# Batch 3's attention begins three steps earlier, and the last output tile is copied by one engine

## The chip, the cores and the metric

The kernel runs on one core of a Trainium2 chip. A core has five engines with a queue each: TensorE (PE in the profile, with PEld for its weight loads), VectorE (DVE), ScalarE (ACT), GpSimd (POOL) and SyncE (SP), which here issues nearly all DMAs. The metric is the device time of one execution in microseconds; shorter is better. What a measurement of this kernel can tell from no change is about 0.2%, some 1.7 us.

## The reference

Three layers in a row: an attention with landmarks (Nystrom) on 4 batches, then two feed-forward layers over 2304 tokens, all in float32.

```python
B, H, S, D = 4, 8, 576, 64              # m = 32 landmarks
q_lm = q.reshape(B, H, m, S // m, D).mean(axis=3)   # k_lm likewise
A, Bm, C = sm(q, k_lm), sm(q_lm, k_lm), sm(q_lm, k) # scaled softmaxes
Z = Bm.T / (norm1(Bm) * norminf(Bm) + 1e-6)
for _ in range(6):
    Z = 2 * Z - Z @ Bm @ Z
x = A @ Z @ C @ v                        # -> 2304 x 512
h = x @ w_in;  x = silu(h) @ w_out       # moe:  512 -> 2048 -> 512
xn = x / rms(x) * rms_g                  # moe2: 512 -> 1536 -> 512
out = (silu(xn @ w_gate) * (xn @ w_val)) @ w_out2
```

## The kernel before

**Precision.** Most matrices are held as a rounded upper part and a remainder (`split`: a cast on ScalarE, a subtraction on VectorE), and one product takes three matmuls.

**First part: 128 steps.** Batch 0 takes steps 0 to 31, and batches 1 to 3 take 32 each: two halves of 288 tokens by 16 blocks of 128 hidden units. A step `i` computes one block's hidden values (`moe1_h`: six matmuls into `h`, then Silu into `s` and the split into `hl`), and three steps later (`LAG`) `retire` multiplies them by the output weights into four PSUM banks `a` (`moe1_out`, twelve matmuls). At the end of a half `moe1_sum` copies these four banks out (tiles `e` and `ex`, by VectorE and ScalarE in turn) and stores them in `x2T`.

**Attention beside it.** While batch b is in its steps, the attention of batch b+1 runs in small pieces, one per step: the generator `attend(ap, b)` lets group 0 (four heads) run alone for `LONE[b]` steps, then both groups together, then six rounds of the iteration for Z (`pe`), then a last small product `pl`, which gives `lts[b]`. `attention(ap, b, g)` holds the pieces of one group; the number of bare `yield`s after `landmarks(kT)` puts off its scores (`pq`, `c1`, `c2`). With `lts[b]` there, `wprime(b, n)` multiplies a quarter n of the input weights by it (`pw` into `wp`), which `moe1_h` uses; it also starts the load of the quarter two further on (`win` from `wind`) into the tile just read. The four `wp` tiles that batch 3's quarters need come free after steps 83, 87, 91 and 95, and a step makes at most one quarter, so each is made in the first such step from the end of the attention on.

**Preparation of the second part.** When the last attention is done, its memory is closed and the pool `p2` opened in its place; the generator `pre` then prepares eight of the twelve weight blocks of the second layer, in the order 1 to 7, 0: load `fw` from `w2d`, four sums `t4` (VectorE), splits into one single-buffered tile `w7p` (ScalarE and VectorE), stores to `w7d` and `wod`. A block takes 12 ticks, and a step gives 2.5 ticks, up to step 125 (the loop's `PRE_REST`); what is left is emitted after the loop (`finish(pre)`). Block 0 is not reloaded: the first step of the second part multiplies by `w7p` itself. Beside it `conversion` turns raw float64 weights into `w2d` (until about step 94).

**Second part: 36 steps.** `moe2_step` does seven products of six matmuls (`ga`, `gb`, `gc`), and between them the output products `o` of the step before (`out_tile`), with weights `oc` loaded by `load_wo2`; `load_split` loads the block `w7` of a later step, `load_f32` the raw block `fw` of one that `late` prepares (8 to 11). The last step's six tiles are copied from PSUM and stored by `out_tile` and `store_out`.

The order of instructions on each engine is made by the framework's scheduler from the order of the code, priorities and buffers, so a moved generator also moves others.

Of the kernel before, what the change touches and what calls it, by code (L numbers as in the profile page):

```python
# [18 lines left out]
P = 128  # L19
B, H, S, D = 4, 8, 576, 64  # L20
# [3 lines left out]
DM = H * D  # L24
# [7 lines left out]
TB = 384  # L32
# [35 lines left out]
LOAD_AT = {3: "o8", 4: "o9", 5: "o10", 6: "n30", 7: "n31", 8: "o11", 9: "o12", 10: "o13", 11: "o14", 12: "o15"}  # L68
CONV_AT = {5: "n20", 6: "n21", 7: "o4", 8: "o5", 9: "o6", 10: "o7", 11: "n30", 12: "n31",
           13: "o8", 14: "o9", 15: "o10", 16: "o11", 17: "o12", 18: "o13", 19: "o14", 20: "o15"}  # L70
NEXT, NEXT0 = 5, 13
FAST_AT = 20
PRE_N = 8
PRE_STEPS, PRE_RATE = 12, 2.5
# [2 lines left out]
NORM_END = 9  # L77
XSPLIT = (0, 3, 6, 9, 12, 15, 18)
LOW = 9
LONE = (0, 6, 8, 8)  # L80


@with_exitstack
def nystrom_moe_kernel(ctx: ExitStack, tc: tile.TileContext, q, k, v, w_in, w_out, w_gate, w_val, w_out2, rms_g, out):
    nc = tc.nc
    PE, DVE, ACT, POOL, SP = nc.tensor, nc.vector, nc.scalar, nc.gpsimd, nc.sync
# [68 lines left out]
    def nslot(i, name, shape, dt=F32):  # L155

        return nw.tile(list(shape), dt, tag=f"n{i}", name=name, bufs=1)
# [54 lines left out]
    def tile_at(n):  # L212
        return (n + NF - CUT) % NF
# [89 lines left out]
    class Queue:  # L303

        last = {}
# [372 lines left out]
    def attention(ap, b, g):  # L678


        n = f"{b}_{g}"
# [35 lines left out]
        yield  # L717
        landmarks(kT)
        yield
        for _ in range((0, 0, 2, 1)[b]):  # L720
            yield

        sa = ht("sa", [P, R, M])
# [29 lines left out]
        with tc.issue_after(now[-1][0].ins):  # L753
            x = AE.activation(ec[:, w1:], c2[:, :nc2], AF.Exp, bias=nb[:, 0:1], scale=0.125 / R, accum_out=su[:, 1:2])
# [9 lines left out]
        last = VE.transpose(bb[:, 1], bb[:, 0])  # L764
# [48 lines left out]
    def attend(ap, b):  # L813


        gens = [attention(ap, b, g) for g in range(NG)]
        for _ in range(LONE[b]):
            next(gens[0])
# [38 lines left out]
    def wprime(b, nb_, prio=0):  # L857


        t = wslot(f"wp_{b}_{nb_}", [P, NG, 2, 512], F32R)  # L860
        pw = [ps(f"pw_{b}_{nb_}_{g}") for g in range(NG)]
        x = []
        if b == 0:
            x = [h_mm[0], *(win_ins["W{0}{1}0"] + win_ins["W{0}{1}1"] if nb_ == 0 else [win_ins[g, nb_] for g in range(NG)])]
        for i in range(4):
            for g in range(NG):
                hr = slice(64 * g, 64 * g + 64)
                with ExitStack() as es:
                    es.enter_context(tc.high_priority(offset=prio))
                    for y in x:  # L870
                        es.enter_context(tc.issue_after(y.ins))
                    PE.matmul(pw[g][32 * i:32 * i + 32], lts[b][hr, i], win_t[i // 2, nb_][hr, i % 2], start=True, stop=True)  # L872
        with tc.high_priority(offset=prio):
            for g in range(NG):
                x = ACT.copy(t[:, g, 0], pw[g])
                y = DVE.tensor_tensor(t[:, g, 1], pw[g], t[:, g, 0].bitcast(F32), op=ALU.subtract)
        wpr[b, nb_] = t

        if b and (b < B - 1 or nb_ < 2):
            n = (nb_ + 2) % 4  # L880
            for g in range(NG):
                win_t[g, n] = nslot(2 * (n % 2) + g, f"win_{g}_{n}_{b}", [P, 2, 512])
                SP.dma_start(out=win_t[g, n].rearrange("p c f -> p (c f)"), in_=wind[g, n])
        return x, y
# [148 lines left out]
    def moe1_h(b, hf, f, c):  # L1033
        ph = ps(f"h_{b}_{hf}_{f}", [P, HB])
        nb_, fo = f // 4, (f % 4) * P
        tk = slice(HB * hf, HB * hf + HB)
        i = 0
        for g in range(NG):
            w, a = wpr[b, nb_][:, g], at_t[b, g]
            for (x, y) in ((0, 0), (0, 1), (1, 0)):  # L1040
                h_mm[0] = PE.matmul(ph, w[:, x, fo:fo + P], a[:, y, tk], start=i == 0, stop=i == 5)  # L1041
                i += 1
        if whole(b, hf, c):
            s = hp.tile([P, 2, HB], F32, tag="hl", name=f"s_{b}_{hf}_{f}")[:, 0]
            x = QA.activation(s, ph, AF.Silu) if f >= NF - CUT else ACT.activation(s, ph, AF.Silu)
            return s, (x, x)
        s = st.tile([P, HB], F32, tag="s", name=f"s_{b}_{hf}_{f}")
        ACT.activation(s, ph, AF.Silu)  # L1048
        hl = hp.tile([P, 2, HB], F32R, tag="hl", name=f"hl_{b}_{hf}_{f}")
        return hl, split(hl, s, lo=DVE)  # L1050
# [126 lines left out]
    def store_out(e, row, last):  # L1177

        for h in range(2):
            y = slice(64 * h, 64 * h + 64)  # L1180
            (SP, POOL)[h and last].dma_start(out=out[row + 64 * h:row + 64 * h + 64], in_=e[y])

    nx = {}

# [80 lines left out]
    oacc = {}  # L1265

    def out_tile(prev, n):

        if prev is None:
            return  # L1270
        p, f, hls, w = prev
        j, t = 1 - n // 3, n % 3
        if f == 0:
            oacc[n] = po.tile([P, DM], F32, tag="o", name=f"o_{p}_{n}", bufs=6)
        for i, (x, y) in enumerate(((0, 0), (0, 1), (1, 0))):
            PE.matmul(oacc[n], hls[j][:, x, t * P:(t + 1) * P], w[:, y], start=f == 0 and i == 0, stop=f == NF2 - 1 and i == 2)  # L1276
        if f == NF2 - 1:
            e = nslot(n, f"e2_{p}_{n}", [P, DM])
            row = (2 * p + j) * TB + t * P
            last = 0 if p < NB2 // 2 - 1 else 1 + n // 5  # L1280
            if last < 2:
                (DVE.tensor_copy if n % 2 else ACT.copy)(e, oacc[n])
                store_out(e, row, last)
            else:
                e2 = nslot(n + 1, f"e2_{p}_{n}_1", [P, DM])
                half = DM // 2
                for eng, fn, t, x in ((POOL, DVE.tensor_copy, e, slice(0, half)), (ACT, ACT.copy, e2, slice(half, DM))):
                    fn(t[:, x], oacc[n][:, x])
                    eng.dma_start(out=out[row:row + P, x], in_=t[:, x])

    def pg(name, tag):
        return pp.tile([P, TB], F32, tag=tag, name=name, bufs=1)
# [2 lines left out]
    def run(gens, n=1):  # L1295
        for _ in range(n):
            for gn in list(gens):
                if next(gn, gens) is gens:
                    gens.remove(gn)
# [41 lines left out]
    pend, gens = [], []  # L1341
# [3 lines left out]
    def ready(b):  # L1345
        return all((b, g) in l_t for g in range(NG))
# [17 lines left out]
    nxt = 1  # L1364
# [16 lines left out]
    for i, (b, hf, f, c) in enumerate(steps):  # L1381
        while hf == 0 and (b, f // 4) not in wpr:
            if not ready(b):
                run(gens)
            else:
                wpfree -= b > 0
                wprime(*todo.pop(0))
        hl, cuts = moe1_h(b, hf, f, c)
        pend.append((steps[i], hl))
        if i + 1 < len(HEAD):  # L1390
            go(HEAD[i + 1])
        if c and f == tile_at(NF - 1):
            es_t[b, hf, c] = sum_tiles(b, hf, c)
        now.append(cuts)
        if not gens and nxt < B and i + NEXT >= 32 * (nxt - 1) + (NEXT0 if nxt == 1 else 0):
            gens = [attend(ap, nxt)]
            nxt += 1
        if gens:
            run(gens, 2 if FAST_AT <= i < 32 else 1)
        if len(pend) > LAG:  # L1400
            retire()
        if hf == 1 and f % 4 == 3:
            wpfree += b < B - 1
        if b == 0:
            if i in LOAD_AT:
                load_job(LOAD_AT[i])
            after = wprime(*todo.pop(0), WP_PRIO) if i in WP_AT else ()
            if i in CONV_AT:
                with behind((*cuts, *after)):
                    finish(jobs.pop(CONV_AT[i]))  # L1410
            if i in KEEP_AT:
                with tc.issue_after(loads.last.ins):
                    keep_win(KEEP_AT.index(i))
        if 0 <= i - SPLIT_AT < NF:
            with behind(cuts):
                split_wout(i - SPLIT_AT)
        if todo and todo[0][0] >= max(b, 1) and ready(todo[0][0]) and wpfree and not (jobs and todo[0][0] > b):
            wpfree -= 1
            wprime(*todo.pop(0))
        if nxt == B and not gens and p2 is None:  # L1420
            att.close()
            p2 = ctx.enter_context(tc.tile_pool(name="p2", bufs=1, side="right"))
        if i >= CONV2_AT:
            due[0] += CONV2_RATE
        if p2 and i < len(steps) - PRE_REST:
            due[1] += PRE_RATE
        with tc.issue_after(cuts[0].ins), tc.issue_after(cuts[1].ins):
            for j, gn in enumerate((conv2, pre)):
                while due[j] >= 1:
                    due[j] -= 1  # L1430
                    next(gn, None)
        if p7 and 1 not in w7_t7:
            w7_t7.append(1)
            load_split(1)
        if p3x and len(x0) > 2:
            finish(norm0)
            split_x(0, x0.pop(0))
        if b == B - 1 and not todo:
            for _ in range(1 + (i % 3 > 0)):
                next(norm0, None)  # L1440
# [17 lines left out]
    for p in range(NB2 // 2):  # L1458
        nxt = p + 1 if p + 1 < NB2 // 2 else None
# [76 lines left out]
```

## Time and profile before

| | |
|---|---|
| median of 3 runs | 847.08 us (845.92 to 847.38) |
| profiled execution: its time, and the span of its instructions | 846.0 us, 843.9 us |
| PE busy | 819.6 us (97%), 6200 matmuls |
| DVE, ACT, POOL busy | 528.6 (63%), 440.3 (52%), 16.2 us (2%) |
| mean granted TensorE clock | 0.992 |
| DMA | 202.89 MB, mean 240 GB/s |

Busy times are sums over the span of 843.9 us; 2.1 us of the execution lie around it. An engine's share is an average over parts with different limits, so the parts are read one by one.

### The profile page before, as it was taken

Reading aid. Unit: us, or ns where it says so; the run is one execution under the profiler, and the core shown is the slowest. Engines: PE = TensorE matmul, PEld = TensorE weight load, DVE = VectorE, ACT = ScalarE, POOL = GpSimd, SP = SyncE. Lnnn points to the kernel's source line nnn. Section 1 sums busy time; section 2 is a strip of 40 time slices with the busy share of each in tenths; the row PEclk is TensorE's granted clock in tenths of the full one; section 3 lists DMA queues with packets and bytes.
Section 4 is the critical chain, followed back from the end, with each engine's and each line's share of the span. In section 5 each row is a group of like instructions: output and inputs, shape, how many; then the busy total and the mean of one; then the engine's idle time right before and its main releaser. Section 6 shows DMA issues by size and latency. Waiting matters only on the chain.

```text
span 843.9 us, 15909 instructions
## 1 busy us (share of the span) xinstructions
PE 819.6 (97%) x6200; PEld 737.5 (87%) x6200; DVE 528.6 (63%) x1111; ACT 440.3 (52%) x929; POOL 16.2 (2%) x46
## 2 busy tenths in 40 slices
PE   8899899999999999999799999999999999999997
PEld 5677678998899979999789999999999999999996
DVE  6988868776589758679544389743458533333332
ACT  4786755785677757667424447433345323232222
POOL 2200000000000000000000000000000000000001
PEclk9999999999999999999989999999999999999999
DMA  9989357478995678868975558668565558555542
GB/s 341 352 298 370 135 170 256 141 219 271 319 307 172 211 252 322 297 247 307 352 262 188 196 191 278 247 229 298 217 224 200 184 188 290 224 221 191 187 186 76
DMA packets 73355, 202.89 MB, mean 240 GB/s; under 512 B 6720, under 2 KB 35008, under 8 KB 69312
## 3 DMA queue, kind: packets, MB, share of 16 engines
q1 hardware_dynamic: 72848, 200.96, 66.7%
q8 instruction: 49, 0.80, 0.4%
q0 software_dynamic: 288, 0.79, 0.3%
q14 instruction: 26, 0.21, 0.1%
q10 hardware_dynamic: 144, 0.13, 0.0%
HBM read 149.29 MB, written 52.56 MB: 239 GB/s over the span
## 4 chain that ended last, share of the span: by engine, by line
PE 88%; DMA 5%; DVE 3%; ACT 2%; SPq 1%; issue 1%; POOL 0%; POOLq 0%; ACTq 0%; DVEq 0%
PE a L1061 18%; PE o L1276 18%; PE ga L1202 18%; PE h L1041 12%; PE gc L1202 9%; PE gb L1202 4%; PE a L1058 4%; PE pw L872 2%; DMA winr<-in_moe_w_in_dram 2%; DMA w7d<-w7p 1%; PE pe L318 1%; DMA win<-wind 1%; DMA fw<-w2d 1%; DMA kT<-in_k_dram 1%; PE pu L301 1%; PE pq L318 1%
## 5 line engine op out<-in xcount | busy, mean ns | idle before, releaser
L1061 PE MATMUL a<-hl,wo 128*128 128x288 f32 x1296 | 194.4, 298 | 0.0
L1061 PEld LDWEIGHTS a<-hl,wo 128*128 128x128 f32 x1296 | 177.7, 188 | 4.3 <-issue 2.1
L1276 PE MATMUL o<-oc,u 128*128 128x512 f32 x648 | 178.9, 394 | 0.0
L1202 PE MATMUL ga<-x,w 128*128 128x384 f32 x840 | 171.9, 339 | 0.0
L1202 PEld LDWEIGHTS ga<-x,w 128*128 128x128 f32 x840 | 152.1, 189 | 12.4 <-ACT a L200 0.2
L1276 PEld LDWEIGHTS o<-oc,u 128*128 128x128 f32 x648 | 119.4, 188 | 13.3 <-DVE u L165 0.3
L1041 PE MATMUL h<-at,wp 128*128 128x288 f32 x768 | 129.9, 305 | 0.2 <-DVE sa L200 0.2
L1041 PEld LDWEIGHTS h<-at,wp 128*128 128x128 f32 x768 | 111.0, 190 | 13.8 <-issue 5.9
L200 DVE TENSOR_TENSOR v<-u,gc 128x384 f32<-128x384 f32 x72 | 39.6, 551 | 124.1 <-PE gc L1202 123.9
L1202 PE MATMUL gc<-x,w 128*128 128x384 f32 x420 | 84.8, 336 | 0.0
L1048 ACT ACTIVATE s<-h 128x288 f32<-128x288 f32 x108 | 44.1, 413 | 75.5 <-PE h L1041 71.3
L1202 PEld LDWEIGHTS gc<-x,w 128*128 128x128 f32 x420 | 75.0, 188 | 2.9
L200 ACT COPY u<-ga 128x384 f32<-128x384 f32 x72 | 34.6, 480 | 73.8 <-PE ga L1202 73.6
L164 ACT CAST u<-u 128x384 fp32r<-128x384 f32 x72 | 37.0, 514 | 66.9 <-DVE u L200 66.9
L200 DVE TENSOR_TENSOR u<-z,v 128x384 f32<-128x384 f32 x72 | 40.1, 556 | 45.7 <-ACT z L200 44.4
L165 DVE TENSOR_TENSOR hl<-s,hl 128x288 fp32r<-128x288 f32 x108 | 48.7, 451 | 25.8 <-ACT hl L164 24.0
L165 DVE TENSOR_TENSOR u<-u,u 128x384 fp32r<-128x384 f32 x72 | 40.0, 556 | 27.1 <-ACT u L164 26.8
L200 ACT ACTIVATE z<-ga 128x384 f32<-128x384 f32 x36 | 17.7, 492 | 69.2 <-PE ga L1202 68.9
L164 ACT CAST hl<-s 128x288 fp32r<-128x288 f32 x108 | 46.8, 433 | 2.6
L1058 PE MATMUL a<-s,wor 128*128 128x288 f32 x160 | 42.5, 409 | 0.8 <-DVE wor L191 0.8
L1202 PE MATMUL gb<-x,w 128*128 128x384 f32 x210 | 42.5, 337 | 0.0
L1058 PEld LDWEIGHTS a<-s,wor 128*128 128x128 f32 x160 | 29.1, 189 | 10.7 <-issue 2.2
(204 smaller groups left out, 931.8 us busy)
## 6 DMA issues: line engine op xcount, KB each, us to landing
w<-w7d SPq DMA_DIRECT2D x31, 1792.0 KB, 7.5
oc<-wod SPq DMA_DIRECT2D x32, 512.0 KB, 7.9
win<-wind SPq DMA_DIRECT2D x20, 512.0 KB, 5.6
w2d<-c SPq DMA_DIRECT2D x36, 256.0 KB, 2.8
fw<-w2d SPq DMA_DIRECT2D x12, 768.0 KB, 6.2
winr<-in_moe_w_in_dram SPq DMA_DIRECT2D x8, 1024.0 KB, 8.1
wor<-in_moe_w_out_dram SPq DMA_DIRECT2D x16, 512.0 KB, 10.3
w7d<-w7p SPq DMA_DIRECT2D x16, 512.0 KB, 5.0
```

The costliest lines, as they stand in the source:

```text
L164: x = ACT.copy(dst[:, 0], src) if hi is ACT else hi.tensor_copy(dst[:, 0], src)
L165: return x, lo.tensor_tensor(dst[:, 1], src, dst[:, 0].bitcast(F32), op=ALU.subtract)
L200: self.last = getattr(self.eng, name)(*args, **kw)
L301: eng.matmul(pu[y], ct[0:VC[c], c, y], vn[0:VC[c], c, h ^ 1], start=c == 0, stop=c == 4)
L318: x = getattr(self.eng, name)(*args, **kw)
L872: PE.matmul(pw[g][32 * i:32 * i + 32], lts[b][hr, i], win_t[i // 2, nb_][hr, i % 2], start=True, stop=True)
L1041: h_mm[0] = PE.matmul(ph, w[:, x, fo:fo + P], a[:, y, tk], start=i == 0, stop=i == 5)
L1048: ACT.activation(s, ph, AF.Silu)
L1058: PE.matmul(acc[d], w[:, y], hl, start=start, stop=stop)
L1061: PE.matmul(acc[d], w[:, x, y], hl[:, z], start=start and i == 0, stop=stop and i == 2)
L1202: mm[0] = PE.matmul(acc, w7[:, x, o, kk], xs[:, y, kk], start=start and n == 0, stop=stop and n == 5, skip_group_check=True)
L1276: PE.matmul(oacc[n], hls[j][:, x, t * P:(t + 1) * P], w[:, y], start=f == 0 and i == 0, stop=f == NF2 - 1 and i == 2)
```

## The change

Batch 3's attention begins at step 56 in place of 59 (a table of starting steps replaces the rule; the entries for batches 1 and 2 are the steps that the rule gave). Its group 1 follows seven steps behind group 0, before eight, and the scores wait one more step. The last of the six output tiles of the last step is copied from PSUM by ScalarE as a whole and stored in two halves of 64 rows by SP's and ScalarE's queues; before, VectorE and ScalarE copied 256 columns each, and GpSimd's and ScalarE's queues stored them.

```diff
-NEXT, NEXT0 = 5, 13
+START = (None, 8, 27, 56)
-LONE = (0, 6, 8, 8)
+LONE = (0, 6, 8, 7)
@@ def attention(ap, b, g):
-        for _ in range((0, 0, 2, 1)[b]):
+        for _ in range((0, 0, 2, 2)[b]):
             yield
@@ def store_out(e, row, last):
-            (SP, POOL)[h and last].dma_start(out=out[row + 64 * h:row + 64 * h + 64], in_=e[y])
+            (SP, POOL, ACT)[h and last].dma_start(out=out[row + 64 * h:row + 64 * h + 64], in_=e[y])
@@ def out_tile(prev, n):
-            row = (2 * p + j) * TB + t * P
             last = 0 if p < NB2 // 2 - 1 else 1 + n // 5
-            if last < 2:
-                (DVE.tensor_copy if n % 2 else ACT.copy)(e, oacc[n])
-                store_out(e, row, last)
-            else:
-                e2 = nslot(n + 1, f"e2_{p}_{n}_1", [P, DM])
-                half = DM // 2
-                for eng, fn, t, x in ((POOL, DVE.tensor_copy, e, slice(0, half)), (ACT, ACT.copy, e2, slice(half, DM))):
-                    fn(t[:, x], oacc[n][:, x])
-                    eng.dma_start(out=out[row:row + P, x], in_=t[:, x])
+            (DVE.tensor_copy if n % 2 and last < 2 else ACT.copy)(e, oacc[n])
+            store_out(e, (2 * p + j) * TB + t * P, last)
@@ the loop over the 128 steps
-        if not gens and nxt < B and i + NEXT >= 32 * (nxt - 1) + (NEXT0 if nxt == 1 else 0):
+        if not gens and nxt < B and i >= START[nxt]:
```

Three places in the order of instructions. The first is VectorE's queue in batch 2's second half, where the first `wp` tiles of batch 3 are made (`hl_2_1_8` is step 88's, `r_` and `c_` are conversion). Before:

```order
L165 TENSOR_TENSOR hl_2_1_9_4326<-s_2_1_9_4324,hl_2_1_9_4326 128x288
L189 SCALAR_TENSOR_TENSOR r_v_11_4167<-r_v_11_4167 128x512
L191 SCALAR_TENSOR_TENSOR c_2028<-c_2028,r_v_11_4167 128x512
L876 TENSOR_TENSOR wp_3_0_4348<-pw_3_0_0_4349,wp_3_0_4348 128x512
L876 TENSOR_TENSOR wp_3_0_4348<-pw_3_0_1_4350,wp_3_0_4348 128x512
L165 TENSOR_TENSOR hl_2_1_10_4384<-s_2_1_10_4382,hl_2_1_10_4384 128x288
```

and now:

```order
L165 TENSOR_TENSOR hl_2_1_6_4241<-s_2_1_6_4239,hl_2_1_6_4241 128x288
L191 SCALAR_TENSOR_TENSOR c_31_4226<-c_31_4226,r_g_10_4075 128x512
L876 TENSOR_TENSOR wp_3_0_4263<-pw_3_0_0_4264,wp_3_0_4263 128x512
L876 TENSOR_TENSOR wp_3_0_4263<-pw_3_0_1_4265,wp_3_0_4263 128x512
L165 TENSOR_TENSOR hl_2_1_7_4293<-s_2_1_7_4291,hl_2_1_7_4293 128x288
```

Quarter 0 of batch 3 has moved by three steps; quarter 2 stands between `hl_2_1_11` and `hl_2_1_12` in both kernels.

The second is SP's queue at the end of the first part: the stores of block 7's and block 0's splits (`w7p_7`, `w7p_0`), the load of block 1 (`w7_1`), of the raw block 8 (`fw_8`), of the next tokens (`xb`), and of the first output weights (`oc_0`). Before:

```order
L954 DMA w7d_90<-w7p_7_5431 256x1x512 x2
L1115 DMA xb_1_0_0_5829<-x2T_87 128x2x384
L957 DMA wod_91<-wop_0_5653 128x1024
L1115 DMA xb_1_0_1_5830<-x2T_87 128x2x384
L954 DMA w7d_90<-w7p_0_5646 256x1x384 x2
L954 DMA w7d_90<-w7p_0_5646 256x1x512 x2
L1090 DMA x2T_87<-e_3_1_0_0_5714 128x288
L1090 DMA x2T_87<-ex_2671 128x288 x3
L1115 DMA xb_1_1_0_5831<-x2T_87 128x2x384
L933 DMA fw_8_6329<-w2d_88 128x1536
L1002 DMA oc_0_5677<-wod_91 128x1024
```

and now:

```order
L954 DMA w7d_90<-w7p_7_5354 256x1x512 x2
L933 DMA fw_8_6329<-w2d_88 128x1536
L1115 DMA xb_1_1_0_5831<-x2T_87 128x2x384
L993 DMA w7_1_5526<-w7d_90 128x3584
L954 DMA w7d_90<-w7p_0_5516 256x1x384 x2
L957 DMA wod_91<-wop_0_5523 128x1024
L954 DMA w7d_90<-w7p_0_5516 256x1x512 x2
L1115 DMA xb_1_0_0_5829<-x2T_87 128x2x384
L1090 DMA x2T_87<-e_3_1_0_0_5714 128x288
L1090 DMA x2T_87<-ex_2671 128x288 x3
L1115 DMA xb_1_0_1_5830<-x2T_87 128x2x384
L933 DMA fw_9_6429<-w2d_88 128x1536
```

The load of `fw_8` has moved from behind the last `x2T` stores to right behind block 7's stores; `w7_1`, which stood ahead of the last two stores of `w7p_7` before, stands behind them; `oc_0` follows `fw_9` now.

The third is VectorE's queue at the change from the first part to the second: `hl_3_1_15` is the last step's split, `t4_8` the sums that read `fw_8`, `e` and `ex` the copies of the last `a` banks, `g1_0`, `v2_0` and `x7_0` belong to the first step of the second part. Before:

```order
L165 TENSOR_TENSOR w7p_0_5646<-t4_0_5580,w7p_0_5646 128x512 x2
L200 TENSOR_TENSOR g1_0_5755<-a1_0_5742,gb_0_5735 128x384
L1175 TENSOR_TENSOR x7_0_5_5744<-xb_0_1_1_4634,x7_0_5_5744 128x384 x2
L1175 TENSOR_TENSOR x7_0_6_5767<-s4_0_5516,x7_0_6_5767 128x384 x2
L942 TENSOR_TENSOR t4_8_6443<-fw_8_6329 128x256 x2
L942 TENSOR_TENSOR t4_8_6443<-fw_8_6329,t4_8_6443 128x256 x2
L200 TENSOR_TENSOR v2_0_5787<-u3_0_5778,gc_0_5780 128x384
```

and now:

```order
L165 TENSOR_TENSOR hl_3_1_15_5643<-s_3_1_15_5641,hl_3_1_15_5643 128x288
L942 TENSOR_TENSOR t4_8_6443<-fw_8_6329 128x256 x2
L942 TENSOR_TENSOR t4_8_6443<-fw_8_6329,t4_8_6443 128x256 x2
L1089 COPY e_3_1_0_0_5714<-a_3_1_0_0_5249 128x288
L1089 COPY ex_2671<-a_3_1_0_2_5251 128x288
L200 TENSOR_TENSOR g1_0_5755<-a1_0_5742,gb_0_5735 128x384
L1175 TENSOR_TENSOR x7_0_5_5744<-xb_0_1_1_4653,x7_0_5_5744 128x384 x2
L1175 TENSOR_TENSOR x7_0_6_5767<-s4_0_5532,x7_0_6_5767 128x384 x2
L200 TENSOR_TENSOR v2_0_5787<-u3_0_5778,gc_0_5780 128x384
```

The four sums on `fw_8` have moved from ahead of `v2_0` to ahead of the last copies; block 0's splits stand much earlier now, two of them (the first on `fw_0`) ahead of `hl_3_1_12`.

## Rows read from the trace of the kernel before

**Rows 1.** Busy time by stage; columns: stretch, length, engines' busy us, clock, DMA share, GB/s.

```profile
320.00:391.00 71.00, 71.00 (x542) 70.00 (x541) 55.76 (x121) 45.40 (x99) 0.00 (x0) 1.00 0.82 294
...
430.00:832.00 402.00, 402.00 (x2089) 373.40 (x2088) 196.66 (x379) 154.72 (x310) 0.00 (x0) 1.00 0.59 215
```

**Rows 2.** Timeline of PE, 304 to 317 us: start, duration, instruction, [idle before, releaser].

```profile
304.08 0.44 PE L318 MATMUL pl<-bbd,ud 128*64 128x128 f32 x4
...
306.23 1.09 PE L872 MATMUL pw<-win,lt 64*32 64x512 f32 x16
...
309.82 1.09 PE L872 MATMUL pw<-win,lt 64*32 64x512 f32 x16
...
314.54 2.22 PE L872 MATMUL pw<-win,lt 64*32 64x512 f32 x16 [1.07 <-DMA win<-wind]
```

**Rows 3.** The four `win` loads between 300 and 330 us: their issue, and time to landing.

```profile
307.81 3.95 SPq L883 DMA_DIRECT2D win<-wind x4
...
DMA to landing us min/median/max: 6.6/7.0/7.4
```

**Rows 4.** Timeline of PE at the first step of the second part.

```profile
409.61 1.21 PE L1202 MATMUL ga<-x,w7p 128*128 128x384 f32 x6
410.65 1.20 PE L1202 MATMUL gb<-x,w7p 128*128 128x384 f32 x6
...
414.31 1.31 PE L1202 MATMUL ga<-x,w7p 128*128 128x384 f32 x6 [1.07 <-ACT u L200]
...
423.95 2.29 PE L1202 MATMUL gc<-x,w7p 128*128 128x384 f32 x6 [6.43 <-DVE v L200]
...
429.15 0.88 PE L1276 MATMUL o<-oc,u 128*128 128x512 f32 x3
```

**Rows 5.** Busy time in short stretches behind that; columns as in the first group.

```profile
417.50:424.00 6.50, 0.07 (x2) 0.05 (x1) 1.98 (x5) 0.49 (x1) 0.00 (x0) 0.80 0.98 376
424.00:426.30 2.30, 2.30 (x7) 2.30 (x8) 0.58 (x2) 0.51 (x1) 0.00 (x0) 0.50 0.74 287
426.30:428.20 1.90, 1.90 (x7) 1.90 (x7) 1.47 (x3) 0.00 (x0) 0.00 (x0) 0.50 0.58 113
```

**Rows 6.** Timeline of DVE in the same place.

```profile
421.88 0.76 DVE L942 TENSOR_TENSOR t<-fw 128x256 f32<-128x256 f32 x2 [7.35 <-DMA fw<-w2d]
```

**Rows 7.** Timeline of SP's DMA queue, 395 to 419 us.

```profile
395.48 0.33 SPq L993 DMA_DIRECT2D w<-w7d x1
...
396.39 1.31 SPq L954 DMA_DIRECT2D w7d<-w7p x2
...
416.58 0.50 SPq L933 DMA_DIRECT2D fw<-w2d x1
417.18 1.53 SPq L1002 DMA_DIRECT2D oc<-wod x3
```

**Rows 8.** Timeline of ACT: block 0's first casts into `w7p`.

```profile
407.82 0.93 ACT L164 CAST w7p<-fw 128x384 fp32r<-128x384 f32 x2 [1.89 <-DMA w7d<-w7p]
```

**Rows 9.** Time to landing of the `oc` loads issued between 417 and 439 us.

```profile
DMA to landing us min/median/max: 5.9/7.2/8.6
```

**Rows 10.** Timeline of DVE: first and last piece of batch 3's score work, group 0.

```profile
241.58 0.47 DVE L200 STREAM_TRANSPOSE sa<-pq 128x288 f32<-128x288 f32 x1
...
245.13 0.21 DVE L200 TENSOR_SCALAR nb<-mx 128x1 f32<-128x1 f32 x1
```

**Rows 11.** End of the execution: timelines of ACT and DVE, and DMA issues with median landing.

```profile
837.01 0.59 ACT L1282 COPY e<-o 128x512 f32<-128x512 f32 x1 [0.92 <-PE o L1276]
837.71 0.42 DVE L1288 COPY e<-o 128x256 f32<-128x256 f32 x1 [0.47 <-PE o L1276]
838.17 0.37 ACT L1288 COPY e<-o 128x256 f32<-128x256 f32 x1 [0.57 <-DVE e L1288]
...
out_dram<-e POOLq DMA_DIRECT2D x6, 128.0 KB, 3.0
...
out_dram<-e ACTq DMA_DIRECT2D x1, 128.0 KB, 3.7
```

## The prediction

> **What bounds the kernel now.** I read the busy time by stage first. From 320 to 391 us PE is busy for 71.00 of 71.00 us, and from 430 to 832 us for 402.00 of 402.00 [rows 1]: in these stretches the matmuls are the time, and a faster neighbour gives nothing. So I looked for the places where PE stands still, in its timeline, and asked of each what ends the wait and whether the change touches it. There are two that it can touch, both at the edge of a stage.
>
> The first is in batch 2's last steps. The reader is to see three `pw` groups in three steps running: at 306.23 and 309.82 us they take 1.09 us, the third, at 314.54, has 1.07 us of idle time before it and takes 2.22 us [rows 2]. The loss is 1.07 + (2.22 - 1.09) = 2.2 us. It waits for the `win` loads, issued from 307.81 us on and landing 6.6 to 7.4 us after their issue [rows 3].
>
> The second is the first step of the second part. Its first product starts at 409.61 us and the next one 1.04 us later; then PE waits 1.07 us for ScalarE and 6.43 us for VectorE's `v`, and the first output product `o` begins at 429.15 [rows 4]. VectorE is not busy in that wait: it stands 7.35 us at the sums on `fw`, until 421.88 [rows 6], because SP issued that load only at 416.58 [rows 7]. The DMAs run at 98% there, and PE leaves the wait at the lower of its two clocks (1.2 GHz in place of 2.4): a granted clock of 0.50 for 2.30 + 1.90 us [rows 5].
>
> **The attention, by steps.** Group 1 needs sixteen calls up to its last piece before the rounds (seven loads and landmarks, one bare yield, eight more), now seventeen. Before, it begins at step 59 + 8 = 67, ends at 82, six rounds fill 83 to 88, and `pl` comes at 89. Now it begins at 56 + 7 = 63, ends at 79, and `pl` comes at 86. So everything that hangs on the end of the attention comes three steps earlier. 542 matmuls in 71 us [rows 1], 18 to a step and 16 of them `pw`, make a step of about 2.4 us; three are 7.3 us.
>
> **Quarter 0 of batch 3** goes from step 89 to 86, quarter 1 from 90 to 87, quarter 2 stays at 91, since its `wp` tile is not free earlier. So the `win` load that quarter 0 sets off has five steps (12 us at least) in place of two. The need is 7.4 us, plus the issue. The 2.2 us go. Bounds: 0 if the queue holds the load up for five steps, 2.2 at best; I take 2.2.
>
> **The preparation.** Ticks from step 89 to 125 are 37 x 2.5 = 92; from step 86 they are 100. Block 0 (the eighth) starts at tick 84 and has its splits at ticks 92 to 96 and its stores at 97 to 101. Before, all of these are left for after the loop; now two stores are. In the trace that remainder stands in SP's queue ahead of the `fw` load that VectorE waits for, and VectorE's order has the sums on it ahead of `v`. Now SP issues this load right behind block 7's stores. Those were issued at 396.39 [rows 7]; 7.3 us earlier is 389, and even with another 9 us for queue and flight the block is there by 398 + 6 = 404, before the sums' new place in the queue behind the last `hl`. So I expect no wait of VectorE for it. What is behind these sums are the copies of the last `a` banks, then `g1_0`, then `v2_0`: if the load were late again, these would be late.
>
> What a first step without these waits takes: seven products at 1.04 us, two more of the next step before `o`, 9.4 us, and some 0.3 us for `u` copies on ScalarE that still come behind its casts (there were 1.07 before). So `o` could start 9.7 us after the first product, where it took 429.15 - 409.61 = 19.5: 9.8 us. They are 7.5 us of waits, 2.1 us of half clock (half of 4.2), and small gaps.
>
> Then the next thing is late: `oc_0`, the weights of that `o`. Its load follows the `x2T` stores, `xb` and `fw_9` in SP's queue, and landing takes 5.9 to 8.6 us [rows 9]. The stores can be issued about 1 us after the first product, so the load goes out some 2.3 us after it and lands at 8.2 to 10.9 us, against a need at 9.7: a wait of 0 to 1.2 us. I take 0.5, and 9.3 us for the whole place. Bounds: 9.8, and 3.3 with a wait of 6.5 us (below).
>
> **What the moved pieces cost in the first part.** The work is the same, three steps earlier, and PE's instructions are the same, so the cost is waits alone. The scores come at step 65, before at 67. There they stood between batch 1's last `a` products and batch 2's first, while VectorE copied the banks; now VectorE has the score work ahead of these copies, and PE has only one `h` between the two. That work took from 241.58 to 245.34 us, 3.8 us with a piece of conversion in it [rows 10]. It can begin two steps (4.8 us) before PE wants the first bank, which leaves about half a microsecond after the copy. I take 0; bounds 0 and 3.8 us, all of it on the path. SP's queue is passed by `vn` and the conversion's loads in another order, within a place or two; products lag three steps behind, which covers it.
>
> **The last tile.** Before, the two half copies come one behind the other (837.71 and 838.17, ending 838.54), since both read one bank; one whole copy by ScalarE takes 0.59 us (the one at 837.01) [rows 11] and would end at about 838.30: 0.24 us less. The stores change queues: GpSimd's landed in 3.0 us, ScalarE's in 3.7 [rows 11], so I count nothing for that and take 0.25; bounds -0.7 (the new ScalarE store later by the difference of these two) and 0.6.
>
> The Trainium skill (DMA: Bandwidth & Descriptors, Specifications) gives a first byte after about 1 us on GpSimd's path and 0.6 on SP's and ScalarE's; by that the end would come, as an estimate, another 0.4 us sooner. The landings above stand the other way round, and the measurement decides.
>
> **Sum.** 2.2 + 9.3 + 0.25 = 11.75 us. The profiled execution took 846.0 us, which makes 834.25. It lies 1.1 us under the median of the runs, 847.08; against the median the forecast is **835.3 us**, with 833 to 837.5 as its own range.
>
> **The rivals.**
> - *`oc_0` is the new wait.* If SP gets to it no earlier than before, 7.6 us after the first product (417.18 against 409.61), it lands at 13.5 to 16.2 us, and PE waits 3.8 to 6.5 us where I took 0.5: 838.6 to 841.3. For it: `fw_9` now stands ahead of it, and the DMAs are full in this stretch [rows 5]. Against it: block 7's stores and `fw_8` have left the stretch. Beside this stands a rule of the Trainium skill (DMA: Bandwidth & Descriptors, Queues, rings and completion order): each DMA engine consumes a queue's descriptors in ring order. By it `oc_0` cannot pass what SP issued before. The rows do not show whether it is so here.
> - *The `win` load is late again*, held behind a conversion load that waits for its buffer: 2.2 us stay, 837.5.
> - *The change does not do what it says*: `fw_8` lands only after the last `a` products, the sums hold the copies, and the wait is back: 835.3 + 9.3 = 844.6.
> - *Slower: the single `w7p` tile.* ScalarE's casts of a block wait until the block before is stored; in its queue they now stand three to four steps (7.3 to 9.7 us) behind the last ones, and the Silu of the running step stands behind them. Before, one such hand-over took 11.4 us (396.39 to 407.82, with 1.89 us of waiting [rows 7, 8]), but `w7_1` was ahead of it in the queue (395.48), which is behind it now. A wait shorter than the lag of three steps, less the 1.6 us that Silu and split take anyway, costs PE nothing. For the kernel to be slower than before, seven hand-overs must lose 1.7 us each (11.75 in all), so each store must take about 8.5 + 5.7 + 1.7 = 16 us. At 18 us the time is about 835.3 + 7 x 3.8 = 862. Against it: from 320 to 391 us the DMAs are busy for 82% only [rows 1], and more overlap with the conversion is confined to three steps.
>
> **The numbers.** Forecast 0.66; `oc_0` 0.12; `win` 0.07; `fw_8` again 0.05; slower hand-overs or score work 0.10. The first three are faster by over 0.2% (1.7 us, which is what a measurement of this kernel can tell from no change), as is most of the fourth (0.03); of the rest 0.04 falls within 0.2% and 0.08 is slower. That is 0.88, 0.04, 0.08. For 8 in 10 the range goes from 832.8 (all bounds at best) to 840.5, which takes in the `win` rival and most of the `oc_0` one.
>
> **What would show it.** Right: no `pw` group over 1.2 us in batch 2's last steps; VectorE's sums on `fw_8` without a wait; the first `o` within 11 us of the first product of the second part; clock 1.00 there. Wrong: an idle PE at `o` with `oc` as its releaser, or at batch 2's first `a`; ScalarE idle before `w7p` casts for several us with Silu behind; or the old 6.43 us wait in another place.

## The result and the profile after

The changed kernel takes **834.71 us** in the median of four runs (834.03 to 834.87), the kernel before 846.74 us in the runs beside them (845.92 to 847.38). The ratio is 0.9857 with a 95% interval of 0.984 to 0.9874: 12 us faster. The forecast was 835.3 us, in a range of 832.8 to 840.5.

The profiled execution has a span of 832.7 us, 11.2 us less than before. Its page, the first part (busy us of each engine, share of the span, instructions):

```profile
span 832.7 us, 15909 instructions
...
PE 817.0 (98%) x6200; PEld 735.2 (88%) x6200; DVE 526.5 (63%) x1110; ACT 440.8 (53%) x929; POOL 15.6 (2%) x45
```

PE's work has not become less (6200 matmuls). Of its busy time 2.6 us have gone: some 2.1 us of matmuls at half clock [rows 4, 5] and 1.1 us of a `pw` group that waited inside [rows 2], less some 0.6 us that came on elsewhere (0.44 of it is a `pw` in the first 125 us, see below). To see where the 11.2 us come from, I cut the span at two instructions that stand in both traces, the first `ga` and the first `o` of the second part:

| stretch | before | after | difference | forecast |
|---|---|---|---|---|
| start to the first `ga` | 409.61 | 408.10 | -1.51 | -2.2 |
| first `ga` to the first `o` | 19.54 | 10.07 | -9.47 | -9.3 |
| first `o` to the end of the span | 414.75 | 414.53 | -0.22 | -0.25 |

For the first stretch, PE's timeline from 299 to 320 us. It answers to [rows 2]:

```profile
299.70 1.09 PE L872 MATMUL pw<-win,lt 64*32 64x512 f32 x16
...
303.33 1.09 PE L872 MATMUL pw<-win,lt 64*32 64x512 f32 x16
...
314.14 1.09 PE L872 MATMUL pw<-win,lt 64*32 64x512 f32 x16
```

The third `pw` has no idle time before it and takes 1.09 us like the others, where it had 1.07 us and took 2.22. SP's queue shows why it has its weights in time. Before, the `win` loads went out at 307.81, 5.7 us ahead of the need, and two `fw` loads stood ahead of them:

```profile
304.64 0.32 SPq L933 DMA_DIRECT2D fw<-w2d x1
...
307.27 0.43 SPq L933 DMA_DIRECT2D fw<-w2d x1
307.81 3.95 SPq L883 DMA_DIRECT2D win<-wind x4
```

Now they go out at 300.82, 13 us ahead of the need, between two `fw` loads. The second fence has their landing, which is no shorter than before (6.6 to 7.4 us [rows 3]):

```profile
298.10 0.32 SPq L933 DMA_DIRECT2D fw<-w2d x1
...
300.82 4.42 SPq L883 DMA_DIRECT2D win<-wind x4
...
306.25 1.46 SPq L933 DMA_DIRECT2D fw<-w2d x1
```

```profile
DMA to landing us min/median/max: 6.4/7.0/7.5
```

For the second stretch, PE's timeline at the first step of the second part, which answers to [rows 4]:

```profile
408.10 1.21 PE L1202 MATMUL ga<-x,w7p 128*128 128x384 f32 x6
409.14 1.20 PE L1202 MATMUL gb<-x,w7p 128*128 128x384 f32 x6
...
413.87 1.32 PE L1202 MATMUL ga<-x,w7p 128*128 128x384 f32 x6 [0.22 <-ACT u L200]
...
418.17 0.86 PE L1276 MATMUL o<-oc,u 128*128 128x512 f32 x3
```

Both waits are gone but for 0.22 us of ScalarE. Windows over the same place (columns as in [rows 1]) show PE busy and its clock at 1.00, against 0.50 in [rows 5]; the DMAs are as full as before:

```profile
407.00:412.00 5.00, 5.00 (x33) 4.79 (x31) 2.41 (x5) 3.06 (x8) 0.00 (x0) 1.00 0.90 294
412.00:418.00 6.00, 5.78 (x33) 5.46 (x33) 3.69 (x7) 2.77 (x7) 0.00 (x0) 1.00 1.03 380
```

VectorE's timeline says what became of the sums on `fw_8` that waited 7.35 us [rows 6]; SP's says when that load went out [rows 7]:

```profile
403.25 0.45 DVE L165 TENSOR_TENSOR hl<-s,hl 128x288 fp32r<-128x288 f32 x1
403.62 0.75 DVE L942 TENSOR_TENSOR t<-fw 128x256 f32<-128x256 f32 x2
404.30 0.88 DVE L942 TENSOR_TENSOR t<-fw,t 128x256 f32<-128x256 f32 x2
407.12 0.46 DVE L1089 COPY e<-a 128x288 f32<-128x288 f32 x1 [1.95 <-PE a L1061]
...
413.85 0.55 DVE L200 TENSOR_TENSOR v<-u,gc 128x384 f32<-128x384 f32 x1 [0.44 <-ACT u L200]
```

```profile
387.68 1.52 SPq L933 DMA_DIRECT2D fw<-w2d x1
...
409.92 0.49 SPq L933 DMA_DIRECT2D fw<-w2d x1
410.51 1.49 SPq L1002 DMA_DIRECT2D oc<-wod x3
```

The load of `fw_8` goes out at 387.68 in place of 416.58. The sums begin at 403.62 without a wait, and VectorE then waits 1.95 us for PE: the order of who waits for whom has turned round.

### The profile page after: what moved, and what is told of

Same layout as the page of the kernel before. It is cut to its first block, busy times and chain, and to the rows that moved or that the text cites. A ratio compares the mean times of both kernels' runs of the same rounds, so it can differ in the third digit from the quotient of the medians.

```text
span 832.7 us, 15909 instructions
## 1 busy us (share of the span) xinstructions
PE 817.0 (98%) x6200; PEld 735.2 (88%) x6200; DVE 526.5 (63%) x1110; ACT 440.8 (53%) x929; POOL 15.6 (2%) x45
## 4 chain that ended last, share of the span: by engine, by line
PE 92%; ACT 3%; DVE 2%; DMA 1%; issue 1%; SPq 0%; POOL 0%; POOLq 0%; ACTq 0%
PE a L1061 20%; PE ga L1202 18%; PE o L1276 18%; PE h L1041 12%; PE gc L1202 9%; PE gb L1202 5%; PE a L1058 4%; PE pw L872 2%; PE pe L318 1%; DMA qT<-in_q_dram 1%; PE pu L301 1%; PE pq L318 1%; ACT L200 0%; PE p L318 0%; PE pm L1140 0%
## 5 line engine op out<-in xcount | busy, mean ns | idle before, releaser
L1276 PEld LDWEIGHTS o<-oc,u 128*128 128x128 f32 x648 | 119.5, 188 | 13.3 <-DVE u L165 0.3
```

## The experiments

**Theory.** The change gains by two loads alone. Where the attention ends three steps earlier, the preparation gets eight more ticks; so little is left for after the loop, the scheduler places `fw_8` and its sums before the change of parts, and `v2_0` no longer stands behind a late load. And the `win` load is there in time. **Rivals:** that the earlier attention or the new order helps by itself; that block 0's leftover (its casts and stores at the change of parts) is the cost and `fw_8` only the last to land; that the load of `win` was late because of what shared the DMAs with it, not because it was asked for late.

All medians, with the two places of each profiled execution (the third `pw`: idle before it, and its duration):

| kernel | median us | third `pw` | first `ga` to first `o` |
|---|---|---|---|
| before | 846.74 | 1.07, 2.22 | 19.54 |
| after | 834.71 | 0, 1.09 | 10.07 |
| hold_pre | 844.36 | 0, 1.09 | 19.58 |
| rate_only | 837.37 | 1.21, 2.22 | 10.07 |
| early_fw8 | 840.42 | 1.27, 2.21 | 13.21 |
| sums_behind | 843.32 | 1.27, 2.22 | 13.68 |
| hold_wp | 835.20 | 0, 1.35 | 10.08 |
| fw_behind | 839.69 | 0, 1.09 | 10.91 |
| fw_behind2 | 836.06 | 0, 1.09 | 10.10 |
| start58 | 835.79 | 0, 1.09 | 10.90 |
| start53 | 835.37 | 0, 1.09 | 10.09 |
| old_tail | 834.65 | 0, 1.09 | 10.07 |

The kernel before ran again beside each group of these: 846.85 us beside hold_pre, rate_only, early_fw8 and hold_wp, 847.64 beside fw_behind, start58, start53 and old_tail, 847.26 beside sums_behind and 847.45 beside fw_behind2. The ratios below are to these, so differences of under 1 us between kernels of different groups are read from the ratios and not from the medians.

**hold_pre: the changed kernel, its preparation held back to step 89.**

```diff
-        if nxt == B and not gens and p2 is None:
+        if nxt == B and not gens and p2 is None and i >= 89:
```

> The changed kernel, with the preparation of the second part's weight blocks held back to step 89, where it began before the change; the attention stays three steps earlier. Theory 1 (the gain is the leftover of block 0 and the fw_8 load behind it, both moved by the ticks won): 92 ticks again, the old wait of VectorE on fw_8 (about 7 us) is back, first ga to first o takes about 19.5 us, time 834.7 + 9.4 = 844.1 us, with no pw wait in batch 2's last steps. Rival (the earlier attention itself or the other order of the first part gives most): 838 us or less.

It took 844.36 us (ratio to before 0.9973, 0.9963 to 0.9983). The whole wait is back, with the same releaser, in PE's timeline:

```profile
409.10 1.21 PE L1202 MATMUL ga<-x,w7p 128*128 128x384 f32 x6
...
423.09 2.29 PE L1202 MATMUL gc<-x,w7p 128*128 128x384 f32 x6 [6.08 <-DVE v L200]
...
428.68 0.88 PE L1276 MATMUL o<-oc,u 128*128 128x512 f32 x3
```

So the earlier attention by itself gives nothing at this place; the ticks do.

**rate_only: the kernel before, with more ticks a step.**

```diff
-PRE_STEPS, PRE_RATE = 12, 2.5
+PRE_STEPS, PRE_RATE = 12, 2.72
```

> The kernel before, attention at step 59 as it was, with 2.72 ticks a step in place of 2.5, so that 37 steps give 100 ticks. Theory 1: first ga to first o takes 10 to 10.5 us, the pw wait of 2.2 us and the old tail stay: 846.7 - 9.4 = 837.3 us. Rival (only an earlier start helps, since the same work in fewer steps makes ScalarE wait for the stores of the single w7p tile): over 841 us.

It took 837.37 us (0.9886, 0.987 to 0.9903), with the attention where it was. One number gives four fifths of the gain. The `pw` wait of the kernel before stays (1.21 us, then 2.22).

**early_fw8: the kernel before, with the load of `fw_8` alone moved up.** It is issued at step 126, ahead of block 0's last stores.

```diff
+        if i == len(steps) - PRE_REST:
+            load_f32(PRE_N)
...
-        if PRE_N <= i + 2 < NF2:
+        if PRE_N < i + 2 < NF2:
             load_f32(i + 2)
```

> The kernel before, with the fw_8 load alone issued earlier, ahead of the last stores of block 0 in SP's queue, and VectorE's sums on it ahead of g1_0; block 0's splits and stores stay behind the first part's last step, and the attention stays at 59. Theory 1a (the load's place in the queue is the cost): the 6.43 us wait and the half clock behind it go, ScalarE's 1.1 us stays, 846.7 - 8 = 838.7 us. Theory 1b (the leftover of block 0, its splits on ScalarE and VectorE and its stores, is the cost, and the load only the last to arrive): 843 us or more.

It took 840.42 us (0.9924, 0.9909 to 0.9939), between the two theories, so the load's place is worth 6.3 us (19.54 to 13.21 us) at least. The other 3.1 us, where I had put 1.1, are ScalarE's wait, what this edit adds, and the lower clock behind both, in PE's timeline:

```profile
414.52 0.61 PE L1202 MATMUL gc<-x,w7p 128*128 128x384 f32 x2 [0.56 <-DVE g L200]
416.26 2.04 PE L1202 MATMUL ga<-x,w7p 128*128 128x384 f32 x6 [1.13 <-ACT u L200]
418.10 1.48 PE L1202 MATMUL gc<-x,w7p 128*128 128x384 f32 x4
```

The sums now stand ahead of `g1_0` and behind block 0's splits, so `gc` waits 0.56 us; then come ScalarE's 1.13 us, and behind these two waits a group of six takes 2.04 us and one of four 1.48, where 1.31 and 0.86 are what they took before, at a granted clock of 0.60 from 416.2 to 418.2 us and 0.50 to 419.4.

**sums_behind: the kernel before, load unchanged, but the sums on `fw_8` behind the first output products, where the program writes them.**

```diff
             if k < 2:
-                sums(i, 2 * k)
-                sums(i, 2 * k + 1)
+                with tc.issue_after(VE.last.ins) if i == PRE_N else ExitStack():
+                    sums(i, 2 * k)
+                    sums(i, 2 * k + 1)
```

> The kernel before, with VectorE's sums on fw_8 put where the program writes them, behind the first output products, instead of ahead of v; the load itself and SP's queue stay as they are. If the 6.43 us wait is only v standing behind these sums in VectorE's order, it goes, and first ga to o would take 10.9 us with ScalarE's 1.07 us left: 846.9 - 8.6 = 838.3 us. But oc_0 is still issued 7.6 us after the first ga and lands 5.9 to 8.6 us later, at 13.5 to 16.2 us, so by the rival of the prediction PE should now stand 2.6 to 5.3 us at o with oc as its releaser: 841 to 843.5 us. I expect the latter. If the load itself held PE in another way, 846 us.

It took 843.32 us (0.9955, 0.9938 to 0.9971). The wait for `v` is gone, with the load as late as ever (issued at 417.36), so PE stood there only because VectorE's order had the sums first. But the next thing was late, in PE's timeline, and the windows behind it show the lower clock (0.50, 1.2 GHz):

```profile
420.54 1.20 PE L1203 MATMUL gb<-x,w 128*128 128x384 f32 x6
424.36 1.44 PE L1277 MATMUL o<-oc,u 128*128 128x512 f32 x3 [2.62 <-DMA oc<-wod]
425.60 2.12 PE L1203 MATMUL ga<-x,w 128*128 128x384 f32 x6
```

```profile
425.60:427.50 1.90, 1.90 (x7) 1.90 (x6) 0.00 (x0) 0.00 (x0) 0.00 (x0) 0.50 1.14 460
```

It is what I expected, and the prediction's first rival, `oc_0` as the new wait, in a kernel where SP gets to that load as late as before: issued 7.3 us after the first `ga` (417.96 against 410.68), PE waits 2.62 us. In the changed kernel it goes out 2.4 us after the first `ga` (410.51), and there is no wait.

**hold_wp: the changed kernel, batch 3's quarter 0 held back to step 89.**

```diff
-        if todo and todo[0][0] >= max(b, 1) and ready(todo[0][0]) and wpfree and not (jobs and todo[0][0] > b):
+        if todo and (todo[0][0] < B - 1 or i >= 89) and todo[0][0] >= max(b, 1) and ready(todo[0][0]) and wpfree and not (jobs and todo[0][0] > b):
```

> The changed kernel, with quarter 0 of batch 3's expert weights held back to step 89 as before the change (quarter 1 at 90), the preparation as changed. Theory 1: the win load of quarter 2 has two steps again, pw waits again and is slow in its rest, 834.7 + 2.2 = 836.9 us, first ga to first o stays at 10 us. Rival (the load was late because of what stood ahead of it in SP's queue or because the DMAs were full, not because it was asked for late): no pw wait, 834.7 us.

It took 835.20 us (0.9858, 0.9844 to 0.9873): the wait did not come back, but for some 0.3 us inside the third `pw` (1.35 us in place of 1.09), and my theory that two steps are too few fell. SP's queue and the landing of these loads:

```profile
298.23 0.32 SPq L933 DMA_DIRECT2D fw<-w2d x1
...
300.62 0.64 SPq L933 DMA_DIRECT2D fw<-w2d x1
...
308.87 1.09 SPq L883 DMA_DIRECT2D win<-wind x2
...
311.76 0.84 SPq L883 DMA_DIRECT2D win<-wind x2
```

```profile
DMA to landing us min/median/max: 4.0/5.0/5.8
```

The load that quarter 2 needs goes out 5.4 us ahead of its `pw` (308.87 against 314.26), no earlier than before (307.81 against 313.47, where the third `pw` could have begun). But these four loads land in 4.0 to 5.8 us and not in 6.6 to 7.4 [rows 3] (the two that quarter 2 needs in 4.0 and 5.0), and both `fw` loads are eight us away, not right ahead of it. So the second theory: what made it late is the two `fw` loads of 768 KB each, issued at 304.64 and 307.27 in the kernel before.

**fw_behind and fw_behind2: the kernel before, with the `fw` loads put behind the `win` loads.** Both have the attention at step 59 and about 100 ticks; fw_behind starts the preparation at step 91 with 2.86 ticks a step, fw_behind2 at 89 with 2.72, as rate_only has it. `last_win` holds the last `win` load that `wprime` has issued so far; the lines that set it, the rate and the starting step are left out here.

```diff
     def load_f32(f):
         fw_t[f] = p2.tile([P, 3 * DM], F32, tag="fw", name=f"fw_{f}", bufs=2)
-        SP.dma_start(out=fw_t[f], in_=w2d[f])
+        with tc.issue_after(last_win[0].ins):
+            SP.dma_start(out=fw_t[f], in_=w2d[f])
```

> The kernel before with attention at step 59, the preparation from step 91 at 2.86 ticks a step (100 ticks), and its fw loads put behind batch 3's last win loads in SP's queue, where before the first two stood ahead of them. The win loads are asked for when they were before. Theory 2 (the wait for win comes from the two fw loads that share the DMAs with it, since with quarter 0 held back but the fw loads eight us away the load landed in 5.0 us and pw did not wait): win lands in about 5 us, pw does not wait, first ga to first o takes about 10 us, 837.4 - 2.0 = 835.4 us. Rival (two steps are too few for that load whatever stands ahead): pw waits about 1 us and is slow, 837.4 us.

> The kernel before, attention at step 59, 2.72 ticks a step from step 89 as in rate_only, and the first fw load put behind the two win loads of quarter 0 in SP's queue (the second behind those of quarter 1). Only this differs from rate_only. Theory 2 (the two fw loads ahead make win late): win lands in about 5 us, no pw wait, and without the hurry that cost 4 us in fw_behind the time is 837.4 - 2.0 = 835.4 us: all of the gain but the tail, with no earlier attention. Rival (win is late because it is asked for late; in fw_behind it was the missing preparation work on VectorE and ScalarE that let pw pass): pw waits, 837.4 us.

In both the third `pw` takes 1.09 us without a wait. The landings of the four `win` loads, first in rate_only, then in fw_behind:

```profile
DMA to landing us min/median/max: 6.6/7.1/7.5
```

```profile
DMA to landing us min/median/max: 3.7/4.3/4.9
```

In fw_behind2 the order of issue and the landings:

```profile
308.89 0.85 SPq L885 DMA_DIRECT2D win<-wind x2
309.84 0.39 SPq L936 DMA_DIRECT2D fw<-w2d x1
312.48 0.80 SPq L885 DMA_DIRECT2D win<-wind x2
```

```profile
DMA to landing us min/median/max: 4.7/5.7/6.9
```

From the first `pw` of batch 3 to the first `ga` fw_behind2 takes 101.68 us (307.77 to 409.45), rate_only 103.55 (307.06 to 410.61): 1.87 us less for the places of two loads in a queue. The two `win` loads that the third `pw` needs, ahead of all `fw` loads now, landed in 4.7 and 5.4 us; the two behind the first `fw` load in 6.0 and 6.9. The Trainium skill (DMA: Bandwidth & Descriptors, Queues, rings and completion order) says that each DMA engine consumes a queue's descriptors in ring order; the landings agree with it, with 6.6 us and more behind two `fw` loads and 3.7 to 5.4 ahead of them. Whether a load ahead delays by its place in the queue or by its share of the DMAs, these runs do not separate. Nor is it a matter of these two alone: with one `fw` load and the conversion's transfers ahead, in one and the same order of issue, the landing took 6.4 to 7.5 us in the changed kernel, 5.7 to 6.8 in old_tail, 5.5 to 6.3 in hold_pre and 5.1 to 6.2 in start53; 13 us of lead hide it in all four.

fw_behind2 took 836.06 us (0.9864, 0.9846 to 0.9882), 0.7 over what I expected; 0.6 of it is the kernel before, which took 847.45 us beside it and 846.85 beside rate_only. It has the attention of the kernel before as a whole (its start, its lead of eight steps and its waits) and the old tail, and stands within 0.1% of the changed kernel's ratio (0.9857). fw_behind took 839.69 us (0.9904, 0.9887 to 0.9921), 4.3 over, 0.8 of it with the kernel before. The rest is the price of the hurry: the same ticks in two steps fewer, and the first `fw` loads 5 us later than in fw_behind2. Its last casts of ScalarE and PE's timeline behind them:

```profile
391.81 0.93 ACT L164 CAST w7p<-fw 128x384 fp32r<-128x384 f32 x2 [3.62 <-DMA w7d<-w7p]
```

```profile
405.83 6.43 PE L1064 MATMUL a<-hl,wo 128*128 128x288 f32 x35 [2.49 <-DVE hl L165]
412.10 1.23 PE L1205 MATMUL ga<-x,w7p 128*128 128x384 f32 x6
```

```profile
405.80:412.10 6.30, 6.27 (x35) 6.27 (x36) 4.19 (x10) 1.25 (x3) 0.00 (x0) 0.73 0.74 274
```

ScalarE waits 3.62 us until the single `w7p` tile is stored, block 0's splits come late, the last steps' `hl` stand behind them in VectorE's queue, and PE waits 2.49 us for one, with a mean clock of 0.73 behind it (0.50 from 408 to 410 us). It is the mechanism of the prediction's slower rival; in the changed kernel, with five steps more for the same ticks, ScalarE's longest wait for such a store is 0.73 us.

**start58 and start53: the changed kernel with the attention begun at step 58, and at 53.**

```diff
-START = (None, 8, 27, 56)
+START = (None, 8, 27, 58)
```

> The changed kernel with START 58 in place of 56, so that the attention ends one step earlier than before the change, not three; 95 ticks, which is all of block 0's splits but one, and none of its stores. Theory 1 (what decides is whether fw_8 and its sums still stand ahead of v behind a leftover; a small leftover puts them behind): little is lost, 0.5 to 1.5 us, 835.2 to 836.2 us. Rival (the gain follows the steps, 12 us for three): 846.8 - 4 = 842.8 us.

> The changed kernel with START 53, three steps earlier still. Theory 1: no wait is left that this can take away, so 834.7 us; if the score work now falls among batch 1's last copies where the changed kernel's did not, up to 3.8 us more. Rival (each step earlier gives some 4 us): 823 us.

start58 took 835.79 us (0.9864, 0.985 to 0.9879), start53 835.37 us (0.9859, 0.9844 to 0.9874). An attention that ends one step earlier than before gives nearly all of the gain, and three steps more than the change give nothing. It is a threshold, not a slope: with 95 ticks block 0's splits are done but for one, and the scheduler now has the load of `fw_8` behind the `oc` loads and the sums on it behind `v2_0`. SP's queue in start58:

```profile
411.40 1.43 SPq L1002 DMA_DIRECT2D oc<-wod x3
...
417.09 0.90 SPq L933 DMA_DIRECT2D fw<-w2d x2
```

What stays is ScalarE's wait of 1.07 us (10.90 us to the first `o` in place of 10.07). It is a matter of ScalarE's order, and not of block 0's splits, which end at 406.5 us: the copy of `u` (411.88) stands behind two casts of `x` (411.07), as in the kernel before (413.79 behind 412.98), and in the changed kernel ahead of them (411.48 ahead of 411.83).

**old_tail: the changed kernel with the tail of before.** The edit puts back the two branches and GpSimd's queue as the diff of the change shows them.

> The changed kernel with the tail of before: the last tile copied in halves by VectorE and ScalarE, stored by GpSimd and ScalarE. By the term of the sum 0.25 us slower, 834.95 us, which is within what a measurement can tell from no change; the last copy begins 0.4 us later, with one half behind the other.

It took 834.65 us (834.44 to 835.55; ratio 0.9852) against 834.71 (0.9857): no difference that can be measured. By the traces the end of the span comes 6.18 us after the last matmul (826.32 to 832.5) with the old tail and 5.96 us (826.74 to 832.7) with the new one.

## Why the prediction was right, point by point

**The first step of the second part: right, in size and mechanism.** 9.47 us came back, 9.3 were forecast. hold_pre and rate_only show from both sides that the ticks decide, sums_behind that the wait was VectorE's order and not the load as such, and early_fw8 how the 9.5 us divide: 6.3 at least for `fw_8`'s place, the rest, 3.1 or less, for ScalarE's wait and the clock (of the 3.1, 0.56 is a wait that the edit itself made). By start58, where ScalarE's wait stands alone, that wait is worth 0.83 us. "So I expect no wait of VectorE for it" was right: the load was expected to go out at 389, at worst with 9 us more; it went out at 387.68 and landed in 7.2 us, at 394.9, 9 us before its sums.

**`oc_0`.** I took 0.5 us; it was 0. The load went out 2.41 us after the first `ga`, where 2.3 was forecast, landed in 6.7 us, at 417.2, and `o` began at 418.17: 1 us to spare. The prediction left open whether a load can pass what SP issued before it. Here it did not: `fw_9`, issued 0.6 us ahead, landed at 415.9. sums_behind shows the rival to be a real one, at a place of SP's queue 5 us later.

**The `pw` wait: right, in size and by the reason given, but that reason is not the only one.** Between the first `pw` of batch 1 (125.10 before, 125.57 after) and the first `ga` the changed kernel gained 1.98 us, which is the 2.2 of the sum but for 0.2. The two loads that the third `pw` needs landed 6.7 and 7.5 us after their issue, no sooner than before (6.6 and 7.4), and were issued 13.3 us ahead, where "five steps (12 us at least)" were forecast. So in the changed kernel it is the lead that took the wait away. Too narrow was "The need is 7.4 us": it is no property of that load. With the `fw` loads elsewhere the same two landed in 4.0 and 5.0 us (hold_wp) or 4.7 and 5.4 (fw_behind2), and two steps did, in hold_wp but for 0.3 us. Either remedy is enough. The prediction's rival for this place named a conversion load ahead of `win`; that the preparation's own `fw` loads stood ahead of it I had not seen, though SP's queue showed them.

**The 0.5 us that the sum did not have** lie in the first 125 us, which the change doesn't touch. A `pw` of sixteen matmuls there took 0.67 us in the kernel before and 1.11 after, at a granted clock of 0.77 and 0.53 in the 1.5 us around it:

```profile
31.56 1.11 PE L318 MATMUL pw<-win,lt 64*32 64x256 f32 x16 [0.41 <-ACT wp L318]
```

```profile
31.50:33.00 1.50, 1.44 (x17) 0.63 (x18) 0.30 (x1) 0.21 (x3) 0.00 (x0) 0.53 0.99 396
```

start58 and old_tail have 1.00 there and 0.67 us: it differs between executions of one and the same instructions.

**The moved pieces in the first part: nothing, as taken.** Where batch 1's last copies now meet the score work, VectorE copies the first bank at 240.98, and PE begins batch 2's products 0.57 us after the end of that copy (about half a microsecond was forecast), without a wait:

```profile
240.98 0.45 DVE L1089 COPY e<-a 128x288 f32<-128x288 f32 x1
```

```profile
242.00 1.79 PE L1061 MATMUL a<-hl,wo 128*128 128x288 f32 x12
```

**The tail: 0.22 us by the traces, 0.25 forecast**, too little for a measurement. The stores' landings were 3.0 us (GpSimd), 3.3 (SP) and 4.2 (ScalarE) in the changed kernel, against the order of the first-byte times that the Trainium skill (DMA: Bandwidth & Descriptors, Specifications) states. In the kernel before, SP's (2.8 us) were ahead of GpSimd's (3.0), and only ScalarE's (3.7) stood against it.

## What to carry to other kernels

Ask of a wait not only which load ended it, but when that load was issued, what stands ahead of that load in its queue and what the waiting engine still has ahead of the instruction that others need: a scheduler that hoists work on a late load to the front of an in-order queue makes a stall out of work that nobody needs yet. A leftover that crosses the border of two stages is a threshold: a small change of rate (here 2.5 to 2.72) or one step of lead did nearly all that could be done there, and more gave nothing. Hurrying the same work into fewer steps has its own price where one buffer is handed from store to cast.

## What was not expected of the hardware

The `win` loads of 512 KB landed in 6.6 to 7.4 us behind two loads of 768 KB issued up to 3.2 us ahead of them in the same queue, and in 3.7 to 4.9 us with none there (fw_behind). With one such load ahead, four traces with one and the same order of issue spread from 5.1 to 7.5 us. The granted clock stayed at 1.00 behind single waits of about 1.1 us at the change of parts (start58, hold_pre) but fell to 0.50 behind one of 2.62 us (sums_behind), behind one of 2.49 us (fw_behind), and behind two of 0.56 and 1.13 us close together (early_fw8). The two long waits so cost PE some 1.7 us more than their length: in sums_behind the three groups behind took 1.44, 2.12 and 1.77 us in place of 0.86, 1.22 and 1.55, in fw_behind 35 matmuls took 6.43 us where 48 take 6.50.
